# Threshold attention and a squared-ReLU MLP in one kernel: weight sums of the MLP shared between VectorE and GpSimd in queues of their own, and PSUM banks not taken right ahead of the attention's values

## The chip, the cores and the metric

The kernel runs on one core of one Trainium2 chip. The metric is the device time of one execution in microseconds (us), lower is better. The kernel before takes 1371.07 us, the median of 3 runs (1367.55 to 1372.39).

## What is computed

Two blocks follow each other. First attention, for 8 batches of 8 heads, 576 positions and 64 features per head, in which only keys whose score is within tau of the row's best take part. Then, with the heads put side by side as 512 features of 4608 tokens, an MLP of 2048 hidden features with a squared ReLU. All in float32.

```python
scores = scale * np.matmul(q, k.transpose(0, 1, 3, 2))
thresh = np.max(scores, axis=-1, keepdims=True) - tau
scores = np.where(scores >= thresh, scores, -1000000000.0)
attn = softmax(scores)                     # written out in the reference
x = np.matmul(attn, v)                     # then (B,H,S,D) -> (B*S, H*D)
...
r = np.maximum(x @ w_in, 0.0)
return (r * r) @ w_out
```

## The kernel before

**Attention.** The work goes in *steps*. A step is one block of 128 query rows of a pair of heads (a *visit* is such a pair; from visit 12 on the visits go two and two, nine steps for two of them, the 64 left-over rows of both in a step of their own). In step s TensorE makes the scores (`scores`, L249) in the two PSUM tiles s0 and s1, of which there is only one each, VectorE takes each row's maximum (L271), ScalarE the exponents (L287), VectorE sets those under the threshold to zero and sums (L299), and GpSimd divides (`divide`, L307 and L309). One step later VectorE turns the weights in 32 by 32 squares into the buffer `turned`, which has two halves (`turn_blocks`, L389), and copies issued by SyncE put the squares into place in wT (`place_blocks`, L401 and L406): 16 for each pair of query blocks. Four steps after a visit's last block, `values` calls `mix`: 20 matmuls (L451) of wT with the values vs, in two PSUM banks; ScalarE evicts them into xT (`put`, L434 to L445). The scores of a step can start only when the threshold of the step before has read s0 and s1.

**MLP.** 256 tokens are a *chunk*. For chunks 2 and later the first layer is a scheme with seven products of half-sized factors instead of eight: `unit` is one product with 8 matmuls (L602) and `product` one half of a second-layer product with 4 (L703). The factors of the units `6`, `5` and `3` are sums of weight blocks (`factor_sum`, L538): `6` is A22 - S3, `5` is that plus A11, `3` is A12 minus the first. There are two column halves q of each and two parts c, so 12 sums of 128x512 for each chunk. They are made anew each time, in places borrowed from g and gsum (`home`). S3 itself is made once, at chunk 1 (L573). The units stand in the order `1 2 5 6 1' 3 7 2' 6' 4 5' 7'`, then the first product, then `3' 4'`; the dash marks q = 1.

**Banks.** PSUM's four banks 4 to 7 are shared by units, products and values. `next_bank` takes the one whose use lies back longest of those not kept. Units `1`, `2` and `5` and the first half of each product take a bank and keep it until `free`. `values` needs two: while more than two are kept, it first runs further pieces of the MLP.

**Order.** All of it is written out by hand: `fill` puts as many pieces (units and half products, 1.76 us each by its own reckoning) between the steps as a rate asks for. `after` emits what follows a piece on other engines (evictions, additions) one piece later. `ask` puts wanted sums into one deque `later`, `some_later` takes the next one and emits it, always on VectorE; `demand` empties the deque up to a wanted sum. The four sums of `6` and `5` with q = 0 are emitted on GpSimd directly, behind the products 6 and 7 of the chunk before (L731, L737). Loads of q, k and v go through a deque too, one or two at a time (`some_loads`), from step 43 on all issued by GpSimd (L193).

```python
"6": (block_of("A22", q, c), block_of("S3", q, c), ALU.subtract),
...
def values(*what):
    if len(kept) > 2:
        after()
    while len(kept) > 2:
        piece()
    mix(*what)
```

Of the kernel before, what the change touches and what calls it, by code (L numbers as in the profile page):

```python
# [12 lines left out]
ALU = mybir.AluOpType  # L13
# [6 lines left out]
def kernel(  # L20
# [10 lines left out]
    nc = tc.nc  # L31
    B, H, S, D = q.shape
    d_model, d_ff = moe_w_in.shape
    n_tokens = out.shape[0]
    P = 128
    HP = H // 2
    NPAIR = B * HP
    NBLK = S // P
# [117 lines left out]
    loads = deque()  # L156
# [41 lines left out]
    def load_v(n):  # L198
        b, h = divmod(visits[n][0], HP)
        h *= 2  # L200
        t = vs[n % 2]
        todo = []
        for u in range(2):
            at = u * (NBLK + 1)
            todo.append((t[:, at:at + NBLK, :], v[b, h + u, 0:NBLK * P, :].rearrange("(c p) d -> p c d", p=P)))
            for half in range(2):
                todo.append((t[half * D:(half + 1) * D, at + NBLK, :], v[b, h + u, NBLK * P:S, :]))
        if paired(n):
            loads.extend(todo)
            return  # L210
        for to, src in todo:
            nc.sync.dma_start(out=to, in_=src)

# [314 lines left out]
    def home(j, p, q):  # L528
        return {("6", 0): ga, ("5", 0): gb, ("3", 0): low, ("6", 1): high, ("5", 1): gb, ("3", 1): high}[p, q]

    def factor_sum(j, p, q, c, engine=None):

        if j >= NCH:
            return
        s2 = home(j, "6", q)[c]
        a, b, op = {"6": (block_of("A22", q, c), block_of("S3", q, c), ALU.subtract), "5": (s2, block_of("A11", q, c), ALU.add),
                    "3": (block_of("A12", q, c), s2, ALU.subtract)}[p]
        (engine or nc.vector).tensor_tensor(out=home(j, p, q)[c], in0=a, in1=b, op=op)  # L538

    def factor(j, p, q, c):  # L540
        where = {"1": "A11", "2": "A12", "7": "S3", "4": "A22"}
# [6 lines left out]
        at = j * TCH % RING  # L548
        return [xT[:, c:c + 2, at + h * P:at + (h + 1) * P] for c in (0, 2) for h in range(2)]

    later = deque()
    asked = set()

    def ask(*what):

        for x in what:
            if x not in asked and x[0] < NCH:
                asked.add(x)
                if x[1][0] == "T":
                    make(*x)  # L560
                else:
                    later.append(x)

    def some_later(count=1):
        for _ in range(min(count, len(later))):
            make(*later.popleft())

    def make(j, p, *rest):

        if p == "S3":  # L570
            q, c = rest
            to = block_of("S3", q, c)
            nc.vector.tensor_tensor(out=to, in0=block_of("A11", q, c), in1=to, op=ALU.subtract)  # L573
        elif p[0] != "T":
            factor_sum(j, p, *rest)
        else:
            x11, x12, x21, x22 = tokens(j)
            to, a, b = {"T1": (T1, x12, x11), "T2": (T2, x22, T1), "T3": (x12, x22, x12), "T4": (T4, x21, T2)}[p]
            nc.gpsimd.tensor_tensor(out=to, in0=a, in1=b, op=ALU.subtract)

    def demand(*what):
        for x in what:
            assert x in asked
            while x in later:
                some_later()

    def unit(j, p, q):

# [98 lines left out]
    def product(j, x, half):  # L687

        p = PRODUCTS[x]
        if half == 0:  # L690
            used["p"] = keep_bank(p)
        to = used["p"][:, 0:HD]
        if x >= 4 and not half and j + 1 in whole:
            ask((j + 1, "T1"), (j + 1, "T2"), (j + 1, "T3"))
        if sums:
            need = {"5": 4, "6": 8, "4": 12, "7": 16}.get(p, 0)
            some_sums(max(need - 16 + len(sums), 1))
            assert state["free"]
        g0, g1 = g[:, 0:HF, :], g[:, HF:, :]
        left, slot = {"1": (g0[:, :, 0:P], Q00), "5": (gsum[0], FT1), "6": (gsum[1], FT2), "2": (g1[:, :, 0:P], Q10),  # L700
                      "7": (gsum[0], FT3), "4": (g1[:, :, P:], FT4), "3": (gsum[1], Q11)}[p]
        for f in range(half * HF // 2, (half + 1) * HF // 2):
            nc.tensor.matmul(to, left[:, f, :], wo[:, slot, f, :], start=(f == 0), stop=(f == HF - 1))  # L703
        if not half:
            return []

        def halves(fn):
            for lo in (0, HF // 2):
                fn(slice(lo, lo + HF // 2))

        def then():
            add, sub, tt = ALU.add, ALU.subtract, nc.vector.tensor_tensor
            c11, c12, c21, c22 = (osb[:, t, h * HD:(h + 1) * HD] for t, h in ((0, 0), (0, 1), (1, 0), (1, 1)))
            free(p)
            if p == "1":
                nc.scalar.copy(p1s, to)
            elif p == "4":
                nc.scalar.mul(c21, to, -1.0)
            elif p == "2":
                tt(out=c11, in0=to, in1=p1s, op=add)  # L720
            elif p == "5":
                nc.scalar.copy(p5s, to)
                halves(lambda f: tt(out=gsum[0][:, f, :], in0=g0[:, f, 0:P], in1=g0[:, f, P:], op=sub))
            elif p == "6":
                tt(out=p1s, in0=to, in1=p1s, op=add)
                nc.gpsimd.tensor_tensor(out=c12, in0=p5s, in1=p1s, op=add)
                halves(lambda f: tt(out=gsum[1][:, f, :], in0=g1[:, f, 0:P], in1=gsum[1][:, f, :], op=sub))
                if j == SEVEN - 1:
                    demand(*((j, "S3", x, c) for x in range(2) for c in range(2)))
                for c in range(2):  # L730
                    factor_sum(j + 1, "6", 0, c, nc.gpsimd)  # L731
            elif p == "7":
                tt(out=c22, in0=to, in1=p1s, op=add)
                tt(out=c21, in0=c22, in1=c21, op=add)
                nc.gpsimd.tensor_tensor(out=c22, in0=p5s, in1=c22, op=add)
                for c in range(2):
                    factor_sum(j + 1, "5", 0, c, nc.gpsimd)  # L737
                ask((j + 1, "3", 0, 0), (j + 1, "6", 1, 0))
                return [lambda: store_rows(j, 1, 2)]
            else:  # L740
                tt(out=c12, in0=to, in1=c12, op=add)
                ask((j + 1, "3", 0, 1), (j + 1, "6", 1, 1))
                return [lambda: store_rows(j, 0, 1)]
        return [then]
# [9 lines left out]
    def paired(n):  # L754

        return n >= 3 * HP
# [7 lines left out]
    def by_dma(n):  # L764

        return n >= 3 * HP - 1
# [79 lines left out]
    def piece():  # L846
        _, fn, *what = waiting.popleft()
        state["left"] -= PIECE_US
        if fn is mlp_out or what[0] <= PLAIN and what[1] == 0:
            after()  # L850
        then = fn(*what)
        after()
        state["then"] = then
        if state["step"] >= NST:
            some_later()

    def fill(us):
        state["left"] += us
        while waiting and state["left"] >= PIECE_US / 2 and waiting[0][0] <= state["usable"]:
            piece()  # L860
        state["left"] = min(state["left"], PIECE_US)

# [4 lines that stand above are left out]
        while len(kept) > 2:  # L867
            piece()
        mix(*what)


    pieces, left = [], n_pieces
# [68 lines left out]
    for s in range(END + 1):  # L941
# [9 lines left out]
        if on:  # L951
            n, i = steps[s]
            at = visits[n][1].index(i)
            last = at == len(visits[n][1]) - 1
            now = list(range(done, done + pieces[s]))
            done += pieces[s]
            more = n + 1 < len(visits)
            short = n < 2 * HP
            if short and at == 0 and 0 < n + 1 < 2 * HP:
                load_qk(n + 2)  # L960
            elif not short and at == 1 and not by_dma(n):
                load_qk(n + 1)
            if now:
                round_weights(now[0], 0)
            if s != 1:
                scores(s)
                after()
        old = steps[s - 2] if 2 <= s < NST + 2 and not by_dma(steps[s - 2][0]) else None
        at_once = now or old or early()
        lay = on and last and more and not by_dma(n) and s != 1  # L970
# [27 lines left out]
        if s == 0:  # L998
            scores(1)
            prep(1)  # L1000
        smooth = s > first_dma + 2 and s not in mixes
        if smooth:
            some_later()
            after()
        if on:
            threshold(n, i)
# [13 lines left out]
        if smooth:  # L1020
            fill(quarter)
            after()
        if 0 < s <= NST and by_dma(steps[s - 1][0]):
            m, x = steps[s - 1]
            turn_blocks(m, x)
        for what in place_at[s]:
            place_blocks(*what)
        some_loads()
        some_later()
        if not smooth:  # L1030
            fill(quarter)
        some_loads()
        if on and at_once:
            divide(n, i)
        fill(quarter)
        some_later()
        some_loads()
        fill(quarter)
        some_loads()
        if on:  # L1040
            for p in now:
# [40 lines left out]
```

## Time and profile before

| | |
|---|---|
| Time | 1371.07 us, median of 3 (1367.55 to 1372.39) |
| Span of the profiled execution | 1365.2 us, granted TensorE clock 0.994 |
| L538 on GpSimd | 64 sums, mean 1395 and 1436 ns |
| L538 on VectorE | 128 sums: 32 each of 1068, 1083, 869 and 705 ns mean |
| L573 on VectorE (S3) | 4 sums, mean 843 ns |
| L309 on GpSimd (division) | 288 parts, mean 874 and 850 ns |
| L193 on GpSimd, loads of v | 144, mean 633 ns, 90.2 us |
| GpSimd waiting at L307 for VectorE's L299 | 217.9 us, 75 times |

How to read it. A row of the page's groups names line, engine, operation, output and inputs, count, busy time, mean of one, and the idle time of the engine just before. PE is TensorE, DVE VectorE, ACT ScalarE, POOL GpSimd, SP SyncE; a q behind the name means the engine's instruction queue. In a timeline the first number is the start from the span's beginning, the second how long it took, and the bracket, where there is one, how long the engine was idle before and what ended that. Waits for several semaphores are put down to the last one. The last 190 us or so have no attention left: only units and products run there.

### The profile page before, as it was taken

How to read it: one execution, taken by the hardware profiler on the slowest of the kernel's cores; microseconds unless marked ns; L12 is line 12 of the kernel's file. 1: busy time of each engine (PE TensorE's matmuls, PEld its weight loads, DVE VectorE, ACT ScalarE, POOL GpSimd, SP SyncE). 2: the span in 40 equal slices, each digit the busy share in tenths (PEclk: the TensorE clock that was granted, in tenths of full speed). 3: DMA queues.
4: the chain of work that ended last, by engine and by line, in shares of the span. 5: the costliest groups of instructions: out<-in, count | busy, mean ns of one | idle time of the engine just before them, and what ended most of it. 6: DMA issues, size and time to landing. Idle time of an engine off the chain costs nothing.

```text
span 1365.2 us, 26326 instructions
## 1 busy us (share of the span) xinstructions
PE 1318.0 (97%) x9112; PEld 1066.0 (78%) x9112; DVE 1000.8 (73%) x2094; ACT 577.7 (42%) x1309; POOL 921.1 (67%) x1209
## 2 busy tenths in 40 slices
PE   6899999999999999999999999999999999999998
PEld 5676556778787878787877877877878887889997
DVE  6877776988787979687978787878787877633341
ACT  4777674225253534343443434343524353422421
POOL 3679774785967878695859777767785867333241
PEclk7999999999999999999999999999999999999999
DMA  7764531545646556555444555444545454320000
GB/s 153 164 155 114 140 94 30 95 84 94 125 90 111 114 102 123 99 119 88 100 86 99 103 113 106 100 83 100 101 102 98 100 96 102 66 56 1 16 17 16
DMA packets 407892, 128.17 MB, mean 94 GB/s; under 512 B 390832, under 2 KB 396752, under 8 KB 407760
## 3 DMA queue, kind: packets, MB, share of 16 engines
q1 hardware_dynamic: 385632, 95.10, 37.3%
q0 software_dynamic: 19824, 31.11, 8.7%
q8 instruction: 73, 1.20, 0.4%
q10 hardware_dynamic: 2304, 0.29, 0.2%
q14 instruction: 59, 0.48, 0.1%
HBM read 50.59 MB, written 9.44 MB: 44 GB/s over the span
## 4 chain that ended last, share of the span: by engine, by line
PE 78%; DVE 5%; SPq 5%; ACT 4%; POOL 4%; issue 3%; DMA 2%; ACTq 0%; DVEq 0%; POOLq 0%
PE bank L602 28%; PE bank L703 24%; PE s L249 11%; PE bank L451 9%; SPq L401 4%; PE bank L499 3%; PE bank L668 2%; PE bank L349 2%; DVE w L299 1%; DVE st L271 1%; ACT w L287 1%; ACT wT L350 1%; POOL g L538 1%; DMA wT<-turned 1%; DVE turned L389 1%
## 5 line engine op out<-in xcount | busy, mean ns | idle before, releaser
L271 DVE TENSOR_REDUCE st<-s 128x1 f32<-128x576 f32 x286 | 203.2, 749 | 111.0 <-PE s L249 110.8
L299 DVE SCALAR_TENSOR_TENSOR w<-s,st,w 128x576 f32<-128x576 f32 x269 | 208.9, 813 | 68.3 <-ACT w L287 68.2
L309 POOL TENSOR_SCALAR w<-w,st 128x576 f32<-128x576 f32 x269 | 232.8, 874 | 25.0 <-DVE st L302 19.0
L703 PE MATMUL bank<-wo,gsum 128*128 128x256 f32 x1088 | 245.9, 382 | 0.0
L703 PEld LDWEIGHTS bank<-wo,gsum 128*128 128x128 f32 x1088 | 204.0, 190 | 40.1 <-issue 10.0
L284 ACT ACTIVATE st<-st 128x2 f32<-128x2 f32 (+1 forms) x148 | 30.3, 205 | 398.9 <-DVE st L271 398.0
L389 DVE STREAM_TRANSPOSE turned<-w 128x512 f32<-128x512 f32 (+2 forms) x388 | 169.3, 490 | 30.3 <-DMA wT<-turned 26.4
L703 PE MATMUL bank<-wo,g 128*128 128x256 f32 x816 | 186.2, 382 | 0.6 <-ACT xT L434 0.6
L307 POOL TENSOR_SCALAR st<-st 128x2 f32<-128x2 f32 (+1 forms) x148 | 35.5, 240 | 224.1 <-DVE w L299 217.9
L249 PE MATMUL s<-kT,qT 64*128 64x288 f32 x1016 | 169.8, 432 | 17.4 <-DVE w L299 11.8
L602 PE MATMUL bank<-xT,w_in_sb 128*128 128x128 f32 x1536 | 184.2, 276 | 0.0
L287 ACT ACTIVATE w<-s,st 128x576 f32<-128x576 f32 x269 | 183.4, 732 | 0.6 <-issue 0.3
L602 PEld LDWEIGHTS bank<-xT,w_in_sb 128*128 128x128 f32 x1536 | 177.9, 192 | 7.2 <-issue 5.7
L451 PE MATMUL bank<-wT,vs 128*64 128x128 f32 (+7 forms) x1700 | 169.6, 357 | 9.1 <-ACT wT L350 3.9
L703 PEld LDWEIGHTS bank<-wo,g 128*128 128x128 f32 x816 | 151.3, 190 | 28.6 <-issue 8.3
L451 PEld LDWEIGHTS bank<-wT,vs 128*64 128x64 f32 (+1 forms) x1700 | 96.6, 136 | 80.1 <-issue 28.5
L249 PEld LDWEIGHTS s<-kT,qT 64*128 64x128 f32 x1016 | 96.8, 188 | 66.7 <-issue 38.5
L614 DVE TENSOR_TENSOR g<-bank,g 128x512 f32<-128x512 f32 x96 | 65.1, 679 | 56.8 <-PE bank L602 56.8
L602 PE MATMUL bank<-t,g 128*128 128x128 f32 x768 | 95.5, 280 | 6.5 <-POOL g L538 4.3
L602 PEld LDWEIGHTS bank<-t,g 128*128 128x128 f32 x768 | 90.0, 194 | 13.4 <-POOL g L538 6.1
L489 POOL TENSOR_TENSOR gsum<-g 128x512 f32<-128x512 f32 x34 | 45.3, 1332 | 75.5 <-ACT g L611 75.1
L193 POOL DMA_DIRECT2D vs<-in_v_dram x144 | 90.2, 633 | 0.0
(109 smaller groups left out, 1962.6 us busy)
## 6 DMA issues: line engine op xcount, KB each, us to landing
wT<-turned SPq DMA_DIRECT2D x800, 72.0 KB, 2.5
wo<-in_moe_w_in_dram SPq DMA_DIRECT2D x16, 512.0 KB, 4.6
wo<-in_moe_w_out_dram SPq DMA_DIRECT2D x16, 512.0 KB, 3.6
out_dram<-osb POOLq DMA_DIRECT2D x32, 256.0 KB, 2.7
ql<-in_q_dram POOLq DMA_DIRECT2D x96, 72.0 KB, 3.0
wT<-turned SPq DMA_DIRECT2D x192, 36.0 KB, 2.1
kl<-in_k_dram POOLq DMA_DIRECT2D x88, 72.0 KB, 3.4
vs<-in_v_dram POOLq DMA_DIRECT2D x48, 128.0 KB, 3.2
```

The costliest lines, as they stand in the source:

```text
L193: (nc.gpsimd if state["step"] > first_dma + 2 else nc.sync).dma_start(out=to, in_=src)
L249: nc.tensor.matmul(sc[u][to, half, 0:HALF], lhsT, keys[rows, half * HALF:(half + 1) * HALF], start=True, stop=True)
L271: nc.vector.tensor_reduce(out=mx[:, u:u + 1], in_=sc[u][:, :, 0:HALF], axis=AX.XY, op=ALU.max)
L287: nc.scalar.activation(out=w[:, u, :].rearrange("p (h k) -> p h k", h=2), in_=sc[u][:, :, 0:HALF], func=AF.Exp, bias=bias[:, u:u + 1], sca ...
L299: nc.vector.scalar_tensor_tensor(out=wu, in0=sc[u][:, :, 0:HALF], scalar=thr[:, u:u + 1], in1=wu, op0=ALU.is_ge, op1=ALU.mult, accum_out=s ...
L309: nc.gpsimd.tensor_scalar(out=w[:, u, :], in0=w[:, u, :], scalar1=z[:, u:u + 1], scalar2=rcp[:, u:u + 1], op0=ALU.add, op1=ALU.mult)
L389: nc.vector.transpose(wb[:, at:at + k1 - k0, i % 2, :], w[:, u, k0 * 32:k1 * 32].rearrange("p (k q) -> p k q", q=32))
L401: nc.sync.dma_start(out=to[:, :, at:at + 64], in_=wb[rows, j::4, :, :].rearrange("p c u q -> p c (u q)"))
L451: nc.tensor.matmul(ps[u * D:(u + 1) * D, :], vs[n % 2][rows, u * (NBLK + 1) + c, :], wT[rows, NBLK if c == NBLK else u * (NBLK + 1) + c, a ...
L602: nc.tensor.matmul(to[:, f, :], factor(j, p, q, c)[:, f * P:(f + 1) * P], part[:, c, :], start=(p in "125" and f == 0 and c == 0), stop=(p ...
L614: nc.vector.tensor_tensor(out=x, in0=to, in1=x, op=ALU.add)
L703: nc.tensor.matmul(to, left[:, f, :], wo[:, slot, f, :], start=(f == 0), stop=(f == HF - 1))
```

## The change

It has three parts. First, the sums that were asked for in advance get two deques, one for VectorE and one for GpSimd: `6` and `3` with q = 1 stay on VectorE, all others and S3 are made by GpSimd. So GpSimd makes 8 of a chunk's 12 sums instead of 4. Each deque has its own places in a step: GpSimd's right behind the scores, ahead of the division, VectorE's right ahead of the threshold. A sum that needs another engine's sum first calls `demand` for that one. Second, no piece that takes a bank is run as the last one ahead of a values block when two banks are kept already (`fill` with `values_next`), and behind the values block a unit `3` or `4` is drawn forward if a piece that takes a bank stood next. Third, the last 64 keys' values of the two heads of a visit are loaded together: 4 loads for each visit instead of 6.

```diff
+        if paired(n):
+            both = t.rearrange("p (u c) d -> p u c d", u=2)
+            src = v[b, h:h + 2]
+            for u in range(2):
+                loads.append((both[:, u, 0:NBLK, :], src[u, 0:NBLK * P, :].rearrange("(c p) d -> p c d", p=P)))
+            for half in range(2):
+                loads.append((both[half * D:(half + 1) * D, :, NBLK, :], src[:, NBLK * P:S, :].rearrange("u p d -> p u d")))
+            return
...
-        (engine or nc.vector).tensor_tensor(out=home(j, p, q)[c], in0=a, in1=b, op=op)
+        getattr(nc, maker(j, p, q, c)).tensor_tensor(out=home(j, p, q)[c], in0=a, in1=b, op=op)
...
-    later = deque()
+    later = {"vector": deque(), "gpsimd": deque()}
+    def maker(j, p, *rest):
+        return "vector" if p in ("6", "3") and rest[0] == 1 else "gpsimd"
...
-            nc.vector.tensor_tensor(out=to, in0=block_of("A11", q, c), in1=to, op=ALU.subtract)
+            nc.gpsimd.tensor_tensor(out=to, in0=block_of("A11", q, c), in1=to, op=ALU.subtract)
         elif p[0] != "T":
+            if p in "35" and rest[0] == 1:
+                demand((j, {"3": "5", "5": "6"}[p], *rest))
...
-            some_later()
+            some_later("vector")
+            some_later("gpsimd")
+
+    def takes_bank(fn, *what):
+        return fn is unit and what[1] in "125" or fn is product and what[2] == 0
+
+    def fill(us, values_next=False):
         state["left"] += us
         while waiting and state["left"] >= PIECE_US / 2 and waiting[0][0] <= state["usable"]:
+            if values_next and len(kept) == 2 and takes_bank(*waiting[0][1:]):
+                break
             piece()
...
         mix(*what)
+        if len(kept) == 2 and len(waiting) > 2 and takes_bank(*waiting[0][1:]) and waiting[2][1] is unit and waiting[2][3] in "34":
+            after()
+            waiting.insert(0, waiting[2])
+            del waiting[3]
...
                 scores(s)
                 after()
+                some_later("gpsimd")
...
+        some_later("vector")
+        some_later("gpsimd")
         if smooth:
-            some_later()
             after()
...
             fill(quarter)
             after()
+            some_later("gpsimd")
...
         some_loads()
-        some_later()
+        some_later("vector")
         if not smooth:
+            some_later("gpsimd")
             fill(quarter)
...
         fill(quarter)
-        some_later()
         some_loads()
-        fill(quarter)
+        fill(quarter, s + 1 in mixes)
```

## The prediction

> **What bounds the kernel now.** I read the page first, then the sums by stretch of 50 us, the waits of TensorE, the waits of SyncE's queue, and the timelines around each gap. Busy shares and the chain of work that ended last:
>
> ```profile
> PE 1318.0 (97%) x9112; PEld 1066.0 (78%) x9112; DVE 1000.8 (73%) x2094; ACT 577.7 (42%) x1309; POOL 921.1 (67%) x1209
> PE 78%; DVE 5%; SPq 5%; ACT 4%; POOL 4%; issue 3%; DMA 2%; ACTq 0%; DVEq 0%; POOLq 0%
> ```
>
> TensorE sets the end: it is busy 97%, the chain is 78% TensorE, and from 1150 us on each stretch has it busy 50.00 of 50. The change removes no matmul, so all it can give or take lies in TensorE's gaps (some 47 us in all), and some 25 us of them lie before 250 us, ahead of every edit (sums by stretch); 19 us are left. TensorE's waits name the rest:
>
> ```profile
> PE s L249 <- DVE w L299: 13.0, 11, 3.9
> PE bank L602 <- POOL g L538: 4.3, 6, 1.2
> PE bank L602 <- ACT g L622: 2.0, 1, 2.0
> PE bank L602 <- ACT g L631: 1.7, 1, 1.7
> ```
>
> Columns: total us, times, longest. Recorded gaps understate what is lost, [...]so below I take start-to-start distances in TensorE's timeline and subtract the usual ones: 1.79 us for a unit (8 matmuls of L602), 1.17 for scores (L249), 4.72 for a values block (L451), 1.82 to 1.93 for half a product (L703) ahead of scores.
>
> **A chain that repeats every 73 us.** From 357 to 584 us, four times:
>
> ```profile
> 358.04 4.25 PE L451 MATMUL bank<-wT,vs 128*64 128x256 f32 x36 [0.67 <-issue]
> 364.94 1.94 PE L249 MATMUL s<-kT,qT 64*128 64x288 f32 x8 [0.73 <-DVE w L299]
> ...
> 358.00 1.50 DVE L389 STREAM_TRANSPOSE turned<-w 128x576 f32<-128x576 f32 x3 [4.43 <-DMA wT<-turned]
> ...
> SPq L401 <- PE bank L451: 40.7, 4, 10.4
> ```
>
> The last line is SyncE's waits from 300 to 600 us: four times, 10 us each, its queue stands at a copy into wT until the previous values block (L451) has read wT. That block is late by choice of the schedule: three banks were kept, so `values` ran two pieces first (half product and unit, 3.7 us: 325.17 to 328.88). The queue then issues its copies back to back, 0.66 us each, up to 355; `turned` comes free late, VectorE stands 4.43 us at L389, the max, the exponents and the threshold behind it are late, and so are the next values and scores.
>
> [...]
>
> **Part by part.**
>
> *No third bank ahead of values.* In the four places above the values block now follows the scores at once, 3.7 us earlier. Its inputs have landed: the last copies it needs landed at 324.0, 397.4, 471.1, 543.8, and it would start at 325.2, 398.9, 472.3, 545.4. SyncE's copies start 3.7 us earlier, so L389 waits 0.7 instead of 4.4. What that is worth: next values block 5.61, 5.81, 5.12, 5.37 minus 4.72 each = 3.0; scores starting 2.73, 2.73, 2.80, 2.73 after the half product instead of 1.93 = 3.3; the scores themselves 1.87 instead of 1.17, four times = 2.8. Sum 9.1 us. Elsewhere: at 895 a product took a bank just written by the values block (5.40 instead of 4.72), now a unit stands between: 0.7 gained; at 742 a unit that takes a bank now follows the values block directly: 0.7 lost by the same measure; at 937 the unit that waited for GpSimd's L538 now comes after the values block: 0.40 + 1.09 = 1.5 gained.
>
> *Sums moved to GpSimd.* Per chunk VectorE loses four sums, 2 of 869 ns and 2 of 705 ns, 16 chunks, and once four of 843 ns: 53 us. None of it is on the path by itself; it counts where VectorE's queue holds the max (L271). At 264 us two S3 sums (1.18 + 0.68) stand ahead of the transposition that scores wait for (3.70 instead of 1.82): 1.9 gained. At 303 us two sums of 0.68 ahead of the threshold (2.83 instead of 1.88, and 1.87 instead of 1.17): 1.65 gained. At 668 two sums (2.3 us) hold the max, ScalarE stands at the exponents, and a unit waits for its copy (L631): 3.69 instead of 1.79, 1.9 gained. At 801 likewise (L622): 3.92 instead of 1.79, 2.1 gained. Sum 7.6 us.
>
> GpSimd gains 64 sums of 1.42 us and four S3 of 1.4: 96 us. They are put ahead of the division, where GpSimd waits for VectorE anyway (217.9 us, 75 times, 2.9 each). The wait added is at the units `3` and `5'`: they need GpSimd's sums. Behind a late sum stand the division, the loads and T4; the division is wanted by L389 a step later. The tightest chunks: at 801 the sums of `5` end at 801.2; then one new sum 1.4, loads 2.7, a store 0.6, the second new sum 1.4: 807.3, wanted at 808.0. At 660, division to 662.1, store 0.6, sum 1.4, five loads 2.7, T4 0.7, store 0.6, sum 1.4: 669.6, wanted at 670.1. Half a microsecond to spare, so some chunks will wait. Lower bound nothing; upper bound both new sums, 2.8 us, in all 12 chunks beside attention, 34 us. I take 3.5 us.
>
> *Last keys' values together.* Two loads less per visit, 48 in all. A load of 64 rows costs GpSimd 549 ns and one of 512 rows 800, so 128 rows are an estimated 585: 24 us off GpSimd, about 2 per chunk, and one load less ahead of L538 at 1006: 0.55 gained on TensorE. GpSimd's net is +72 us; beside attention from 73% to about 78%.
>
> Sum: 9.1 + 0.7 - 0.7 + 1.5 + 7.6 + 0.55 - 3.5 = 15.2 us. From 1371.07: 1356.
>
> **Rivals.**
> - *GpSimd becomes the bound of the chunk starts* (slower). For it: 0.5 us to spare, L538 waits in three chunks already. Against: GpSimd's 2.9 us waits, and idle 27% beside attention. If each of 12 chunks waits 2.8 us and VectorE then stands for the division, 34 us lost against 18.7 won: about 1385. Chance 8%.
> - *The gain is hidden elsewhere*: SyncE's 0.66 us per copy, not the wait, sets the copies' end, or other waits take the place of those removed. Then some 2 us remain: 1369. For it: 40 copies per visit at 0.66 are 26 us of some 36 us. Against: the 10 us stops are a plain wait. Chance 12%.
> - *Only the values part pays*; GpSimd gives back what VectorE's relief won: 9 us, 1362. Chance 25%.
> - *No new waits at all*, and the half-full VectorE removes the small qT and wT waits too: 21 us, 1350. Chance 15%.
>
> **How the numbers follow.** The likeliest, 40%: 1356. The range 1348 to 1368 takes in all but the slower rival, part of "hidden" and the far end of the best case. Faster by over 0.3% (below 1367): 40 + 25 + 15 and a little of the hidden case, 0.82. Within: 0.10. Slower: 0.08.
>
> **What would show it.** Right: SyncE's 10 us waits on L451 shrink to about 6; no DVE wait of 4.4 us at L389 from 350 to 580; no L249 wait on L299 at the repeating places; L631 and L622 gaps gone; POOL busy near 990, DVE near 948. Wrong: more TensorE time waiting for POOL L538 (then GpSimd is late), or L602 and L451 waiting for L434/L438 after values blocks. The prediction falls if what TensorE loses after 250 us, start to start, is not some 15 us smaller.

## The result, and the profile after

The changed kernel takes 1352.5 us (median of 4 runs, 1350.85 to 1353.89), the kernel before 1371.73 in the same comparison (4 runs, 1367.55 to 1375.45): ratio 0.9865, 95% interval 0.984 to 0.989, so 19 us less. The prediction of 1356 was 3.5 us above it, the direction was right and the range held the time.

Busy time and chain of the profiled execution, whose span fell from 1365.2 to 1352.1 us:

```profile
PE 1314.7 (97%) x9112; PEld 1062.1 (79%) x9112; DVE 953.0 (70%) x2026; ACT 578.6 (43%) x1309; POOL 972.6 (72%) x1229
PE 83%; DVE 5%; POOL 4%; ACT 3%; issue 2%; SPq 1%; DMA 1%; ACTq 0%; DVEq 0%; POOLq 0%
```

TensorE's work is the same 9112 matmuls; VectorE has 48 us less and GpSimd, which also issues fewer loads, 51.5 more. SyncE's share of the chain went from 5% to 1%. The waits of TensorE (total us, times, longest) show which ones ended:

```profile
PE s L254 <- DVE w L304: 9.2, 6, 3.9
PE bank L612 <- POOL g L543: 2.6, 3, 1.2
PE bank L456 <- ACT w L292: 2.1, 1, 2.1
PE bank L612 <- POOL t L589: 1.4, 2, 1.1
...
PE bank L612 <- ACT g L632: 0.3, 1, 0.3
```

The scores' wait for the threshold (L249 before, L254 now) fell from 13.0 us in 11 times to 9.2 in 6, and of the two waits of 1.7 and 2.0 us for ScalarE's copies 0.3 is left. One wait is new, that of a values block, put down to ScalarE's exponents (2.1); and the units' wait for `t` grew from 0.2 to 1.4. That is T1 (L589), a difference of two token blocks which GpSimd makes for unit `5`. The repeating place, whose lines of before are in the prediction, now runs through without a wait (timeline of TensorE):

```profile
358.02 1.24 PE L254 MATMUL s<-kT,qT 64*128 64x288 f32 x8
359.19 4.79 PE L456 MATMUL bank<-wT,vs 128*64 128x320 f32 x40
363.90 1.99 PE L713 MATMUL bank<-wo,gsum 128*128 128x256 f32 x8
365.83 1.24 PE L254 MATMUL s<-kT,qT 64*128 64x288 f32 x8
```

Scores follow the half product after 1.93 us instead of 2.73, and take 1.17 until the next one. The waits of SyncE's queue from 300 to 600 us:

```profile
SPq L406 <- DVE turned L394: 25.5, 9, 5.4
SPq L406 <- PE bank L456: 24.1, 4, 9.0
SPq L411 <- PE bank L456: 20.0, 4, 5.3
```

SyncE's four stops at L406 (L401 before) went from 40.7 to 24.1 us: the first, at 331 us behind a late values block, is still 9.0, the other three 4.8 to 5.2. The four at L411 are the copies of left-over rows, which now come so early that they too meet a values block still to run; in the timelines nobody waits for them. So SyncE stands no less for values blocks in all (42.2 us before, 44.1 now); what shrank are the stops of the copies on which `turned` hangs. VectorE's stop at the same place is still there, at half its length, and TensorE has no wait behind it:

```profile
357.84 1.50 DVE L394 STREAM_TRANSPOSE turned<-w 128x576 f32<-128x576 f32 x3 [2.26 <-DMA wT<-turned]
```

**Where the 13 us of the spans came from.** Below is the start of the same step's scores, after minus before, as worked out from both timelines.

| up to | after minus before, us | what happened on the way |
|---|---|---|
| 266 us | -1.7 | S3 sums no longer ahead of scores: -1.9 |
| 290 | -0.4 | a values block comes before its copies have landed: +1.2 |
| 343 | +2.6 | +0.3 a wait for `t`; -0.7 sums no longer ahead of a threshold (303 us); +3.5 the values block at 322.55 (below) |
| 414 | +0.2 | first period: -2.3 |
| 485 | -2.6 | second: -2.8 |
| 556 | -4.5 | third: -1.9 |
| 579 | -5.9 | fourth: -1.4 |
| 666 | -7.7 | +0.2 on the way; two sums no longer ahead of the maximum: -2.0 |
| 677 | -7.0 | a unit waits for GpSimd's sum: +0.7 |
| 747 | -6.3 | a product takes a bank just written by values: +0.7 |
| 799 | -8.0 | as at 666: -1.7 |
| 938 | -10.2 | -0.6 at 895 us, -1.5 at 930 |
| 1008 to the end | -13.1 | -2.7, of which about 1.4 is the clock (below) |

The row at 343 us holds the largest loss, and its lines in TensorE's timeline are:

```profile
321.38 1.24 PE L254 MATMUL s<-kT,qT 64*128 64x288 f32 x8
322.55 0.76 PE L456 MATMUL bank<-wT,vs 128*64 128x320 f32 x4
325.38 5.88 PE L456 MATMUL bank<-wT,vs 128*64 128x256 f32 x36 [2.08 <-ACT w L292]
```

Four matmuls run, then the block stands 2.08 us. The release is put down to ScalarE's exponents, but those of the step that it reads had long ended. What the block needs are SyncE's copies, whose last one landed at 324.88; in the run with the sums of 5 made earlier the same wait is put down to these copies (last section). SyncE's queue (start, length, instructions) leaves little room for them to be sooner, 32 of them being issued almost without a stop, 0.72 us each:

```profile
298.55 23.09 SPq L406 DMA_DIRECT2D wT<-turned  x32
```

Then the 36 matmuls take 5.88 us instead of 4.25: the sums by stretch (busy us of each engine, then granted clock, share of the DMA engines and GB/s) have half the clock for 3.4 us.

```profile
321.00:325.30 4.30, 2.31 (x16) 1.14 (x15) 3.81 (x7) 1.05 (x4) 4.13 (x6) 1.00 0.49 103
325.30:328.70 3.40, 3.32 (x14) 1.91 (x16) 3.31 (x10) 0.60 (x1) 3.07 (x5) 0.50 0.00 0
328.70:332.00 3.30, 3.30 (x31) 1.96 (x28) 0.79 (x3) 0.67 (x4) 0.36 (x1) 1.00 0.00 0
```

The profile of before has one such stretch too, from 1011.8 us, after two waits for GpSimd. The medians differ by 19 us where these two profiles differ by 13: the one of before lies low among its runs (it took 1367.0), the one of after is the slowest of its four (1353.89). The time of a kernel goes roughly with its granted clock (before: 1368.05 us in a run at 0.995, 1376.64 at 0.989).

### The profile page after: what moved, and what is told of

The parts are those of the page before. It is cut to its first block, busy times and chain, and to the rows that moved or that the text cites. A ratio compares the mean times of both kernels' runs of the same rounds, so it can differ in the third digit from the quotient of the medians.

```text
span 1352.1 us, 26266 instructions
## 1 busy us (share of the span) xinstructions
PE 1314.7 (97%) x9112; PEld 1062.1 (79%) x9112; DVE 953.0 (70%) x2026; ACT 578.6 (43%) x1309; POOL 972.6 (72%) x1229
## 4 chain that ended last, share of the span: by engine, by line
PE 83%; DVE 5%; POOL 4%; ACT 3%; issue 2%; SPq 1%; DMA 1%; ACTq 0%; DVEq 0%; POOLq 0%
PE bank L612 28%; PE bank L713 26%; PE s L254 12%; PE bank L456 10%; PE bank L504 3%; PE bank L678 2%; PE bank L354 2%; POOL g L543 1%; DVE st L276 1%; DVE w L304 1%; ACT wT L355 1%; ACT w L292 1%; SPq L406 1%; POOL w L314 1%; DVE turned L394 1%
## 5 line engine op out<-in xcount | busy, mean ns | idle before, releaser
L314 POOL TENSOR_SCALAR w<-w,st 128x576 f32<-128x576 f32 x269 | 227.1, 854 | 22.9 <-DVE st L307 15.5
L394 DVE STREAM_TRANSPOSE turned<-w 128x512 f32<-128x512 f32 (+2 forms) x388 | 169.7, 491 | 21.5 <-DMA wT<-turned 19.9
L254 PE MATMUL s<-kT,qT 64*128 64x288 f32 x1016 | 167.5, 433 | 11.0 <-DVE w L304 8.0
L312 POOL TENSOR_SCALAR st<-st 128x2 f32<-128x2 f32 (+1 forms) x148 | 34.4, 232 | 180.3 <-DVE w L304 172.4
L254 PEld LDWEIGHTS s<-kT,qT 64*128 64x128 f32 x1016 | 95.7, 188 | 57.2 <-issue 31.0
L621 ACT ACTIVATE g<-g 128x512 f32<-128x512 f32 x128 | 80.7, 631 | 4.1
```

What stands on the lines that cost most here:

```text
L254: nc.tensor.matmul(sc[u][to, half, 0:HALF], lhsT, keys[rows, half * HALF:(half + 1) * HALF], start=True, stop=True)
L314: nc.gpsimd.tensor_scalar(out=w[:, u, :], in0=w[:, u, :], scalar1=z[:, u:u + 1], scalar2=rcp[:, u:u + 1], op0=ALU.add, op1=ALU.mult)
L394: nc.vector.transpose(wb[:, at:at + k1 - k0, i % 2, :], w[:, u, k0 * 32:k1 * 32].rearrange("p (k q) -> p k q", q=32))
L621: nc.scalar.activation(out=to, in_=to, func=AF.Square)
```

## The experiments

Theory at the outset: the values part carries two thirds of the gain, through SyncE's copies; the sums give some 4 us net; the loads next to nothing; and what the profile of after lost at 325 us can be had back. Rivals: the sums carry the gain, or VectorE's relief makes the copies come in time. Each kernel was timed in five rounds beside the kernel before. The median of before was 1370.42 us with the first four kernels below, 1370.47 with the next four and 1368.67 with the last four; so kernels are compared by their ratios, where a thousandth is 1.4 us.

### The values part alone

```diff
 (kernel before)
-    def fill(us):
+    def fill(us, values_next=False):
...
+            if values_next and len(kept) == 2 and takes_bank(*waiting[0][1:]):
+                break
...
         mix(*what)
+        if len(kept) == 2 and ... and waiting[2][3] in "34":
+            after()
+            waiting.insert(0, waiting[2])
+            del waiting[3]
```

> The kernel before with the second part of the change alone: no third bank ahead of a values block, and the unit 3 or 4 drawn forward behind it. Theory (the values block that comes 3.7 us late holds SyncE's copies, and through the buffer turned the max, the exponents and the next scores): 9.1 us at the four repeating places, 1.5 at the values block near 937 us, 0.7 won and 0.7 lost elsewhere: 10 to 11 us faster than before, near 1361, and no VectorE wait of 4 us at the turning (L389) from 350 to 580 us. Rival (SyncE's rate of 0.66 us per copy sets the copies' end, so the waits come back elsewhere): at most 2 us faster. Rival (the relief of VectorE did it): no change beyond 1 us.

Measured: 1358.56 us, ratio 0.9915 (0.9897 to 0.9932), 11.7 us less. The waits of SyncE from 300 to 600 us:

```profile
SPq L401 <- DVE turned L389: 30.5, 12, 6.2
SPq L406 <- PE bank L451: 20.9, 4, 5.4
SPq L401 <- PE bank L451: 20.4, 4, 5.1
```

The four stops of 10 us are 5 us here, with every sum still where it was. So the chain of values block, copies, `turned` and maximum is confirmed, and it is the larger part. (Of the scores' waits for the threshold at these places one is left, 1.32 us at 434.96, with half a clock behind it: 16 matmuls of a product from 437.07 take 5.13 us, 3.72 elsewhere. The two halves of this part, holding a piece back and drawing a unit forward, were not run apart.) What belongs to the sums is untouched (waits of TensorE):

```profile
PE bank L602 <- ACT g L622: 2.0, 1, 2.0
PE bank L602 <- ACT g L631: 1.7, 1, 1.7
```

### The sums alone

```diff
 (kernel before)
-    later = deque()
+    later = {"vector": deque(), "gpsimd": deque()}
+    def maker(j, p, *rest):
+        return "vector" if p in ("6", "3") and rest[0] == 1 else "gpsimd"
 ... and the places of some_later("gpsimd") and some_later("vector") as in the change
```

> The kernel before with the first part alone: the sums shared out in two deques, S3 on GpSimd. Theory: 7.6 us of waits behind VectorE's queue go, some 3.5 us of new waits for GpSimd come, and where SyncE's copies set the pace a part is given back: 3 to 6 us faster, the four repeating waits of about 4 us at the turning stay. Rival (GpSimd becomes the bound): slower than before by up to 15 us. Rival (all of the gain is VectorE's): 15 us or more faster.

Measured: 1369.28 us, ratio 0.9988 (0.9978 to 0.9998), 1.6 us less where 3 to 6 were expected. The stops of SyncE's queue stay (its waits from 300 to 600 us):

```profile
SPq L401 <- PE bank L451: 42.2, 4, 10.8
```

At a place where before had no wait, unit `3` now waits for GpSimd's sum (timeline of TensorE):

```profile
740.32 1.83 PE L607 MATMUL bank<-xT,gsum 128*128 128x128 f32 x14 [1.15 <-POOL gsum L538]
```

Step by step the gains are there (1.9 at 266, 2.0 at 666, 1.7 at 800 us), and waits take nearly all of it back: +1.3 at 290, +1.2 for `t` at 595, +0.9 at 677, +1.4 at 740, +1.8 at 870 for a transposition of keys.

### The loads alone

```diff
 (kernel before; and the old path for paired visits goes)
+        if paired(n):
+            ...
+            for half in range(2):
+                loads.append((both[half * D:(half + 1) * D, :, NBLK, :], src[:, NBLK * P:S, :].rearrange("u p d -> p u d")))
+            return
```

> The kernel before with the third part alone: the last 64 keys' values of both heads in one load, 48 loads of GpSimd fewer. Theory: 24 us less on GpSimd, on TensorE 0.5 us or so: the same within 2 us. Rival (GpSimd is the hidden bound of the chunk starts): 3 to 5 us faster.

Measured: 1371.36 us, ratio 1.0004 (0.9993 to 1.0015): no difference, with GpSimd's busy time down from 921.1 to 900.3 us. In this kernel, where TensorE waits for GpSimd's sums 4.3 us in all, 21 us of GpSimd's time are worth nothing that can be measured.

### Unit 3' ahead of the values block

The changed kernel loses most where a values block comes before its copies. This puts a unit of 1.79 us in front of it instead of behind.

```diff
 (changed kernel)
-        mix(*what)
-        if len(kept) == 2 and ... and waiting[2][3] in "34":
+        if len(kept) == 2 and ... and waiting[2][3] in "34":
             after()
             waiting.insert(0, waiting[2])
             del waiting[3]
+            piece()
+        mix(*what)
```

> The changed kernel, but the unit 3 of the second half that is drawn forward runs ahead of the values block instead of behind it, so five values blocks come 1.8 us later, no third bank is taken. In the changed kernel the first of the four moved values blocks waits 2.1 us for copies into wT (they land at 324.9, TensorE stands there at 322.5) and TensorE's clock is halved for 3.4 us after it. Theory (the delay of a values block has some 2.9 us of slack in SyncE's chain, of 3.7 us in the kernel before only the excess was paid): the wait and the half clock go, about 3 to 4 us faster than the changed kernel, no waits of scores for the threshold at the repeating places. Rival (every microsecond that a values block is late is paid): 1.8 us lost at each of three or four places, 3 to 5 us slower than the changed kernel.

Measured: 1360.34 us, ratio 0.9925 (0.9909 to 0.9941): 8 us slower than the changed kernel where 3 to 4 less were expected. The wait at 325 us did go (2.8 us less there). But at two of the five places the unit now waits for VectorE's sum which it reads, and at all five the product behind the values block takes a bank that this block has just filled (0.6 to 0.7 us each; timeline of TensorE):

```profile
395.78 1.83 PE L612 MATMUL bank<-xT,gsum 128*128 128x128 f32 x14 [0.99 <-DVE gsum L543]
...
403.00 1.99 PE L713 MATMUL bank<-wo,g 128*128 128x256 f32 x8 [0.68 <-ACT xT L439]
...
891.05 3.36 PE L612 MATMUL bank<-xT,gsum 128*128 128x128 f32 x14 [2.29 <-DVE gsum L543]
```

The last one costs 5.0 us in all, since its wait of 2.29 is again followed by half a clock (3.36 us for 14 matmuls, 1.83 elsewhere). Step by step 1.0 to 5.0 us are lost at each of the other four places: the idea was right at one of five.

### The change without the values part

```diff
 (changed kernel: fill, values and the last call of fill as in the kernel before)
```

> The kernel before with the first and the third part (sums shared out, values of the last keys together), without the bank rules. With the sums alone new waits came: a unit 3 for GpSimd's sum (1.1 us at 740), T1 at 595 (1.4), the key transposition at 870 (0.4). Theory (GpSimd's time is what the sums alone lack, the loads give it back): those waits shrink, 2 to 4 us faster than the sums alone, 1366. Rival (the bank rules are what makes room for the sums, by moving the values block ahead of the units that need the sums): within 1 us of the sums alone, 1369.

Measured: 1364.94 us, ratio 0.9959 (0.9947 to 0.9972). That is 4.0 us better than the sums alone (0.9988), although the loads alone gave nothing: the wait for the transposed keys at 870 us is gone (-1.8), and at 1008 us it is -2.5. Of the latter 0.8 are shorter waits for GpSimd; the rest goes with half a clock, which the trace of the sums alone has and this one has not (30 matmuls of units from 1013.65 us take 5.24 us there, from 1012.12 us 3.62 here). Adding the values part to this kernel makes the change, so there that part is worth 0.9959 - 0.9865, or 12.9 us.

### The change without the loads

```diff
 (changed kernel: six loads of values for each visit as before)
```

> The changed kernel without its third part: bank rules and shared sums, 48 more loads on GpSimd. Theory (loads give GpSimd the room that the sums take): 2 to 4 us slower than the changed kernel, 1355 to 1356, with more of TensorE's waits for GpSimd's L538. Rival (the bank rules make the room): within 1 us of the changed kernel's 1352.5.

Measured: 1358.07 us, ratio 0.991 (0.9893 to 0.9927), 6.2 us slower than the change where 2 to 4 were expected. The wait for transposed keys, which the sums alone had too, is back:

```profile
860.44 1.19 PE L249 MATMUL s<-kT,qmid 64*64 64x288 f32 x12 [0.42 <-DVE kT L229]
```

Step by step it is 1.8 us there and 0.9 at 1008. But the profiled execution is only 1.0 us longer than that of the change, because the latter holds the half-clock stretch and this one does not. It was also the fastest of its six runs (1354.84). So of some 6 us the traces show 2.7; the rest is not seen in them and stays open.

### GpSimd's sums of 5 made earlier

```diff
 (changed kernel)
                 for c in range(2):
                     factor_sum(j + 1, "6", 0, c)
+                for c in range(2):
+                    factor_sum(j + 1, "5", 0, c)
...
-                for c in range(2):
-                    factor_sum(j + 1, "5", 0, c)
                 ask((j + 1, "3", 0, 0), (j + 1, "6", 1, 0))
```

> The changed kernel, but the two sums of 5 with q = 0 are put into GpSimd's queue right behind those of 6, behind product 6 instead of product 7, so ahead of a division and some loads. Theory (in the changed kernel TensorE waits for these sums at 675, 725 and 1000 us because GpSimd comes to them late, 0.5, 1.2 and 0.9 us): these waits go, 2 to 3 us faster than the changed kernel. Rival (the division pushed back holds VectorE's turning, then the max and the scores): waits of scores for the threshold at the chunk starts, no gain or up to 5 us slower.

Measured: 1352.68 us, ratio 0.9872 (0.9855 to 0.9889): as the change. The rival holds: the units' waits at 725 and 1001 us for these sums are gone, and in place of the first the scores wait, for the threshold behind a division that came later:

```profile
724.68 1.94 PE L254 MATMUL s<-kT,qT 64*128 64x288 f32 x8 [1.77 <-DVE w L304]
```

### Unit 3' ahead of values at chunk 2 alone, and a unit 7 drawn forward

```diff
 (changed kernel)
-        mix(*what)
-        if len(kept) == 2 and ... and waiting[2][3] in "34":
+        forward = len(kept) == 2 and ... and waiting[2][3] in "347"
+        if not forward or waiting[2][2] > SEVEN:
+            mix(*what)
+        if forward:
             after()
             waiting.insert(0, waiting[2])
             del waiting[3]
+            if waiting[0][2] == SEVEN:
+                piece()
+                mix(*what)
```

The `7` in the condition is a second edit: behind one values block, near 730 us, a unit `7` is drawn forward.

> The changed kernel with two edits. At chunk 2 alone the unit 3 of the second half runs ahead of the values block; behind a values block a unit 7 may be drawn forward too, which concerns the block near 730 us alone. Theory: the wait of 2.1 us for the copies into wT at 325 us and the half clock behind it go (2.8 us to the next step in the run with the unit ahead everywhere), and the 0.6 us for the eviction (L439) at 735 us: 3 to 3.5 us faster than the changed kernel, 1349. Rival (SyncE's copies set the pace from 290 us on): the wait comes back at the next values blocks, within 1 us of the changed kernel.

Measured: 1349.66 us (1349.08 to 1351.71), ratio 0.9847 (0.9834 to 0.9859): the lowest ratio of all, 2.5 us better than the change where 3 to 3.5 were expected, though the two intervals overlap. In the trace the first edit is worth 2.6 us and the second 0.7. The timeline of TensorE at the place of the 2.08 us wait:

```profile
322.36 1.24 PE L254 MATMUL s<-kT,qT 64*128 64x288 f32 x8
323.53 2.21 PE L612 MATMUL bank<-xT,gsum 128*128 128x128 f32 x16
325.67 5.06 PE L456 MATMUL bank<-wT,vs 128*64 128x320 f32 x40
331.41 1.99 PE L713 MATMUL bank<-wo,g 128*128 128x256 f32 x8 [0.68 <-ACT xT L439]
```

The block begins when its copies are there, with no wait and at full clock; the bank just written costs 0.68.

### Both amendments

```diff
 (changed kernel with the edits of the two kernels above)
```

> The changed kernel with two amendments at once: at chunk 2 alone unit 3' stands ahead of the values block (alone: 1349.7 us), and GpSimd makes the two sums of 5 with q = 0 right behind those of 6 (alone: 1352.7, as the changed kernel). Theory, that the 1.3 us by which the second one's profile was shorter is real once no other wait falls on it: 1347 to 1348. Rival, that the wait for GpSimd's sum only moves to L304: 1349.7 as with the first alone, between 1349 and 1351.

Measured: 1350.27 us, ratio 0.9866 (0.9847 to 0.9884), not better than with the first amendment alone; by its ratio it is no better than the changed kernel either, so the 2.5 us of the first are not clear of noise. At 723 us the scores wait 1.77 us for the threshold as above, as the rival said, and in this trace half a clock follows (the 40 matmuls of a values block from 725.5 take 6.19 us, 4.79 elsewhere), which the same wait did not have above. The earlier place of the sums of 5 is not shown to be better.

### The values part and the loads

```diff
 (kernel before with the edits of "the values part alone" and "the loads alone")
```

> The kernel before with the second and third parts (banks, loads) and without the first. Theory, that the joint loads pay only where GpSimd makes the additional sums, because only there something waits for GpSimd: within 1.5 us of the second part alone (1358.6), so 1357 to 1360. Rival, that the loads are worth 4 to 5 us wherever the values come in time: 1353 to 1355.

Measured: 1356.97 us, ratio 0.9909 (0.9894 to 0.9924), against 0.9915 for the values part alone. The loads give nothing here either: they pay with the sums, and not because the values come in time.

### Two of GpSimd's sums made twice

```diff
 (changed kernel)
-        getattr(nc, maker(j, p, q, c)).tensor_tensor(...)
+        for _ in range(2 if (p, q) in (("3", 0), ("5", 1)) else 1):
+            getattr(nc, maker(j, p, q, c)).tensor_tensor(...)
```

> The changed kernel with each of GpSimd's sums of 3 (q = 0) and 5 (q = 1) written twice, the same numbers again: four more sums per chunk, 5.6 us of GpSimd's time, some 90 us in all, 65 of them beside attention. Theory, that GpSimd has half a microsecond to spare at the tightest chunk starts, as the prediction said: 2.8 us late in most of the 12 chunks, 10 to 30 us slower, 1362 to 1382. Rival, that its waits of 172 us at the division take the sums in: under 5 us slower, below 1357.5.

Measured: 1396.04 us, ratio 1.0188 (1.0166 to 1.0209), 44 us slower than the change and beyond the theory's end of 30; the rival, under 5 us, is out. GpSimd still waits 141.2 us at the division for VectorE's threshold (172.4 in the change). So that total was no measure of its room: GpSimd can wait 141 us and still hold TensorE up where a sum is wanted at once. Waits of TensorE:

```profile
PE bank L613 <- POOL g L544: 19.8, 7, 4.1
...
PE bank L613 <- POOL gsum L544: 6.8, 4, 2.3
PE bank L613 <- POOL t L590: 6.0, 3, 2.8
```

These three are 32.6 us, against 4.0 for the same causes in the change. The clock adds to it (timeline of TensorE, where these 14 and 16 matmuls take 1.83 and 1.95 us otherwise):

```profile
323.93 3.35 PE L613 MATMUL bank<-t,g 128*128 128x128 f32 x14 [3.92 <-POOL g L544]
327.08 3.29 PE L613 MATMUL bank<-xT,w_in_sb 128*128 128x128 f32 x16
```

Its mean granted clock is 0.987 against 0.994 in the change: from 300 us on its clock record has 24 us at half clock, that of the change 3.4; by the 1.4 to 1.6 us lost in each 3.4 (last section) an estimated 9 of the 44 us are the clock's.

### The sums of 3 back on VectorE

```diff
 (changed kernel)
-        return "vector" if p in ("6", "3") and rest[0] == 1 else "gpsimd"
+        return "vector" if p == "3" or p == "6" and rest[0] == 1 else "gpsimd"
```

> The changed kernel with the two sums of 3 with q = 0 made by VectorE again, so GpSimd makes 6 of 12 sums. Theory, that at 668 and 801 us VectorE's queue holds the row maximum again behind these sums: 3 to 4 us slower, 1355 to 1357. Rival, that either engine has room for two sums when the values come in time: within 1 us of the changed kernel, 1351.5 to 1353.5.

Measured: 1349.72 us (1348.31 to 1350.61), ratio 0.9856 (0.984 to 0.9872): not slower than the change, where 3 to 4 us were expected; by ratio it is 1.2 us faster, which is within the intervals. Both steps at which the theory saw the gain keep it, 2.0 us at 662 and 1.7 at 794. The timeline of VectorE shows why. In the kernel before, two sums stood behind the transposition and ahead of the maximum:

```profile
665.06 0.65 DVE L538 TENSOR_TENSOR gsum<-w_in_sb,g 128x512 f32<-128x512 f32 x1
665.63 1.69 DVE L538 TENSOR_TENSOR gsum<-w_in_sb 128x512 f32<-128x512 f32 x1
667.25 1.41 DVE L271 TENSOR_REDUCE st<-s 128x1 f32<-128x576 f32 x2
```

Here:

```profile
656.10 0.68 DVE L624 TENSOR_TENSOR g<-bank,g 128x512 f32<-128x512 f32 x1
656.70 0.68 DVE L543 TENSOR_TENSOR gsum<-w_in_sb 128x512 f32<-128x512 f32 x1
...
659.96 1.51 DVE L394 STREAM_TRANSPOSE turned<-w 128x512 f32<-128x512 f32 x4
663.28 1.42 DVE L276 TENSOR_REDUCE st<-s 128x1 f32<-128x576 f32 x2 [1.80 <-PE s L254]
```

Both the sums of `3` and those of `6'` are VectorE's here, yet in this step none stands between the transposition and the maximum, which waits for TensorE and no longer the other way round. A sum stands ahead of the threshold. The changed kernel does not put all of VectorE's sums there: a second place behind the transposition is left, of the two that were there before, and one step earlier a sum takes it (at 653.01), but one alone, and the maximum behind it still waits 1.10 us for TensorE. So it was the place of the sums that held the maximum, not that VectorE made them. And GpSimd, relieved of two sums for each chunk, makes others wait less: the wait for `t` at 588 us is gone (-1.1), that for GpSimd's sum at 676 too (-0.7), and the values block of 325 us waits 1.55 us, with no half clock behind it:

```profile
321.56 0.76 PE L456 MATMUL bank<-wT,vs 128*64 128x320 f32 x4
323.87 4.25 PE L456 MATMUL bank<-wT,vs 128*64 128x256 f32 x36 [1.55 <-ACT st L290]
```

Its profiled span is 1347.1 us against 1352.1. This edit and unit 3' ahead at chunk 2 were not run together. Nor was a kernel with all sums left on VectorE and only their places changed, which would say what the move to GpSimd itself is worth.

## Why the prediction was right, and which of its steps were not

| step of the prediction | said | found |
|---|---|---|
| four repeating places | 9.1 us | 8.5 step by step; SyncE's stops at L406 9.0 once and about 5 three times (said: about 6); VectorE's at L394 2.1 to 2.3 (said: 0.7) |
| 937, 895 and 742 us | 1.5 + 0.7 - 0.7 | 1.5 + 0.6 - 0.7 |
| sums at 264, 668, 801 us | 1.9 + 1.9 + 2.1 | 1.9 + 2.0 + 1.7 |
| sums at 303 us | 1.65 | 0.6 at 306, and lost at the next values block |
| loads | 0.55 | 0 alone, 4 to 6 with the sums |
| GpSimd's new waits | -3.5 | about -1.9: T1 at 588 us 1.1 and at 300 us 0.3, sum of 5' 0.47; other waits shrank, so TensorE waits for GpSimd 4.0 us in all, 4.5 before |
| total | 15.2 | 13.1 between the profiles, 19 between the medians |

That the total came so near is in part luck. Between the profiles 4.7 us were lost that nobody forecast (1.2 at 290 us, 3.5 around the values block at 322.55), and against them stand 2.7 us won at 1008 us, half of it clock, and the 3.5 us for GpSimd, of which 1.9 were paid.

**Right: the mechanism of the values part.** It said that a block late by choice of the schedule holds SyncE, and that through `turned` and the maximum it holds TensorE. The values part alone gave 11.7 us, and 12.9 on top of the rest; the prediction's share for it was 9.1 + 1.5 = 10.6. The rival that SyncE's 0.66 us per copy hides the gain fell at the repeating places. That a recorded gap understates the loss shows in the same trace at a unit: the first matmul behind the wait of 1.74 us at 672.05 takes 0.38 us, those from 668.4 to 668.7, which no wait precedes, 0.275 each. That a recorded wait of 0.73 us costs 1.5 at the repeating places has a plain reason in the trace of before: the matmuls into s0 start at 364.94, those into s1 at 365.68, each when its own half of the threshold (0.74 us apart) is done, so the scores take 0.7 us longer too.

**Wrong: "its inputs have landed".** The step took the landing times of before (324.0) and the block's start (325.2) as a slack of 1.2 us and at the same time booked 1.9 and 1.65 us of gain ahead of it. TensorE with these gains stood at the block at 322.55, while the copies, issued back to back, landed at 324.88. So the gains ahead of this place were spent waiting at it, and the clock took 1.6 more: 3.5 us in all. The values part alone, which has none of these gains ahead of it, waits 0.32 us there. The same happened at 290 us (+1.2), where the copies landed at 282.92 and the block had started at 281.96. Here the rival with SyncE's rate was right: gains ahead of a place that a transfer limits don't add to its own. Unit 3' ahead of the block, at chunk 2 alone, took 2.6 of the 3.5 us back in its trace.

**Wrong in size: the loads.** "0.55 gained on TensorE" followed from one load less ahead of one late sum. The loads are worth 0 without the sums (with or without the values part) and 4.0 or 6.2 with them. The estimate of a load of 128 rows was near: 96 loads of 701 ns mean, 48 of them of 512 rows at 800, leave 602 ns against 585. What failed is that it booked the loads apart from the sums: they lower what the sums cost. How they do so is seen only in part: the wait for transposed keys (1.8 us) and shorter waits for GpSimd at 1008 us (0.8). As a pair the two were put at 7.6 - 3.5 + 0.55 = 4.65 us; measured were 5.6 (0.9959) without the values part and 6.9 (0.9915 to 0.9865) with it, so the rival that only the values part pays is out. Each term alone was wrong: the sums gave 1.6 alone where 7.6 - 3.5 = 4.1 were booked.

**Right, with too good a reason: the sums.** The gains at 264, 668 and 801 us came as priced. But of the last two the text said that two sums on VectorE hold the maximum, and took moving them to GpSimd as the cure. With the sums of `3` back on VectorE in their new place the gains stay: the order was the cure.

**Right: little to spare on GpSimd, though not where it was looked for.** That four more sums per chunk cost 44 us shows that GpSimd has little room. But at 801 and 660 us, the chunks reckoned through, the new sums made no unit wait but one for 0.47 us; the largest new wait is at unit `5`, for T1 at 588 us, ahead of which a new sum now stands in GpSimd's queue. The prediction counted what stands behind a late sum, but not T1.

GpSimd's and VectorE's busy times came to 972.6 and 953.0 where 990 and 948 were said. The sums on GpSimd took less than the 1.42 us assumed: means of 1278 to 1387 ns by kind in the group rows. How much longer a sum takes on GpSimd than on VectorE depends on what is compared: by the medians of single sums in the kernel before 1.9 times (1.27 and 0.68 us), by the means of the changed kernel, VectorE's being 1019 and 1079 ns, 1.2 to 1.4 times. The longest single one on VectorE took 2.44 us, at 656.59 in the trace of before, where GpSimd makes sums from 657.21 on.

## What to carry to other kernels

Where one engine's queue holds another's inputs, look first at the order: putting a block 3.7 us earlier, or a sum behind the maximum instead of ahead of it, gave more here than handing two more sums per chunk from the busier VectorE to GpSimd, which gave nothing that can be measured (the sums of 3 back on VectorE). Gains ahead of a place that a transfer limits are not added to the gain at that place (4.7 us were lost so here, at 290 us and at 322.55, 1.6 of them to the clock); recompute the arrival there first. An edit that is worth nothing alone can be worth 4 to 6 us beside another that loads the same engine, so test it in both surroundings.

## What was not expected of the hardware

Short waits can cost TensorE more than themselves. After 2.08 us (at 325), after 2.29 us (unit 3' ahead, at 891), and after two of 1.02 and 1.18 us within 3 us (before, at 1011.8) the granted clock was 0.50 for the next 3.4 us, some 1.4 to 1.6 us lost each. The length of the wait does not decide it: 1.32 us had such a stretch behind it (the values part alone, at 434.96), while 1.98 us (the change without the loads, at 325.04) and 1.92 us had none (the 36 matmuls behind take 4.25 us both times, as elsewhere). The latter, with the sums of 5 made earlier:

```profile
321.59 0.76 PE L456 MATMUL bank<-wT,vs 128*64 128x320 f32 x4
324.27 4.25 PE L456 MATMUL bank<-wT,vs 128*64 128x256 f32 x36 [1.92 <-DMA wT<-turned]
```

The clock records of before and of the change show a pattern. In each of the two traces all changes of the clock lie on a grid of 3.41 us, which starts elsewhere in each; the half clock in the change lasts from 325.30 to 328.71 and that in before from 1011.81 to 1015.23. These are the only such stretches between 100 and 1320 us. TensorE's busy time in all grid intervals between these times in which it is under 2.1 us, and the clock granted in the next interval:

| trace | interval, us | TensorE busy, us | clock in the next |
|---|---|---|---|
| change | 321.89 to 325.30 | 1.42 | 0.50 |
| before | 264.29 to 267.71 | 1.61 | 1.00 |
| before | 803.60 to 807.01 | 1.67 | 1.00 |
| before | 1008.40 to 1011.81 | 1.76 | 0.50 |
| before | 670.48 to 673.89 | 1.84 | 1.00 |
| change | 1007.97 to 1011.38 | 1.99 | 1.00 |
| before | 1022.05 to 1025.47 | 2.00 | 1.00 |

So both stretches stand behind an interval with much idle time, but no limit in busy time parts them from the others: 1.76 us was followed by half clock, 1.61 was not. In neither was TensorE idle throughout. What decides is open. That such a stretch falls in one run and not in the next could explain why the same kernel's time spreads by 3 to 9 us; this is an estimate from the mean clocks (before: 1368.05 us at 0.995, 1376.64 at 0.989) and was not tested by itself.
